# A linear-attention scan and a gated feed-forward layer on one core: v in two transfers, and three PSUM banks for the second layer from its first unit

## The chip, the cores and the metric

One core of a Trainium2 chip. The metric is the device time of one launch in microseconds (us), the median of three runs; lower is better. Five engines are programmed: TensorE (PE, matmuls; its weight loads are PEld), VectorE (DVE), ScalarE (ACT), GpSimd (POOL) and SyncE (SP, which here only issues DMAs). Each engine runs its instructions in the order in which the program gives them to it, and waits on semaphores for the others.

## The reference, cut to what matters

```python
# r, k, v: (4, 8, 768, 48); w, u: (8, 48)
for t in range(S):
    cur = einsum('bhd,bhe->bhde', u * kt, vt)
    y[:, :, t] = einsum('bhd,bhde->bhe', rt, state + cur)
    state = w * state + einsum('bhd,bhe->bhde', kt, vt)
x = y.transpose(0, 2, 1, 3).reshape(4, 768, 384)
h = maximum(x @ w_in, 0)                  # 384 -> 1024
conv_out = 3-tap convolution of h along the sequence, a weight per channel
out = (h * sigmoid(conv_out)) @ w_out     # 1024 -> 384
```

## The kernel before

The scan is done in 24 groups g of 128 tokens (4 batch elements of 6 groups; two chunks of 64 tokens in each). `load(g)` brings k and r with the head dimension on the partitions (tile KR, two transfers of 48 or 64 rows), v with the tokens on the partitions (tile TOK), and from g = 11 (NE) on also k and r with the tokens on the partitions (`in_krt`, into TOK). v lies in memory with zeros beside it, in blocks of [128 rows, 2, 384]; rows 0 to 63 need block 0 and rows 64 to 127 block 1, 1,536 bytes a row. `prep(g)` multiplies KR by decay factors (`TKR`, made once at the start in the PSUM bank PO2; `TKS` is its copy in SBUF), makes the scaled k (for g < 11 by matmuls, line 453) and the diagonal of the scores. `visit(g, av, su)` is the scan itself: scores of the next group (SP, line 516), outer products k by v of the next group (UP, line 525), and outputs of this group (AV, lines 521 and 527). Its outputs go to XT; from g = 3 on, six small SBUF-to-SBUF transfers of a group ("mv", line 560) put the last head in place.

The feed-forward layer goes in seven units u of up to 462 columns, and eight blocks f of 128 channels: `first` makes nine matmuls into HP (line 585), then ACT and DVE do the convolution and the gate, and the result is split into two parts GG (ten buffers). `second` makes three matmuls for each of three output blocks m (line 626), and accumulates over f in the PSUM banks PO0 to PO2. In units u < PH (two of them) only m = 0 and 1 follow each f; m = 2 follows for all eight f at the end of the unit, in bank PO0, since PO2 still holds the decay factors. The weights are converted piece by piece in unit 0 (`convert`: one DMA of 384 KB into one of three staging tiles ST, two ACT steps, one on DVE, one more on ACT, one on DVE or POOL).

The program lists all steps with what they read and write; a planner (`Plan.order`) with a cost for each step and a due time then writes out one order for all engines, and puts matmuls on zeros (line 699, "fillers") into PE gaps that it expects. Most steps go through helpers, so their lines in the profile are 292 (`tt`, an elementwise operation) and 295 (`dma`). Which step it is, is told by the tiles: KR<-KR,PO is the multiplication by the factors in PSUM, KR<-KR,TKR by those in SBUF.

Of the kernel before, what the change touches and what calls it, by code (L numbers as in the profile page):

```python
# [14 lines left out]
B, H, S, D = 4, 8, 768, 48  # L15
DM, DF = 384, 1024
C = 64
NP = H // 2
# [18 lines left out]

NE = 11
NX = 3
GP = 11  # L40
PH = 2
NBUF = 4
NT = 4
NO = 2
# [17 lines left out]
class Plan:  # L62
# [11 lines left out]
    def op(self, eng, dur, rd, wr, fn, cls="", x=0.0, port=False, mode=0, dma=False):  # L74
        n = len(self.ops)
        self.dma.append(dma)
        pred = set()
        for k in rd:
            if k in self.last_w:
                pred.add(self.last_w[k])  # L80
        for k in wr:
            if k in self.last_w:
                pred.add(self.last_w[k])
            pred.update(self.last_r.get(k, ()))
        for k in rd:
            self.last_r.setdefault(k, []).append(n)
        for k in wr:
            self.last_w[k] = n
            self.last_r[k] = []
        pred.discard(n)  # L90
        if not isinstance(dur, dict):
            dur = {eng: dur}
        cls = cls or (wr[0] if isinstance(wr[0], str) else wr[0][0])
        self.ops.append((dur, x, sorted(pred), fn, cls, mode))
        self.port.append(port)
        return n
# [134 lines left out]
def rwkv_ffn_kernel(tc, krd, krt, vt, wd, ut, w_in, conv_w, w_out, out):  # L231
    nc = tc.nc
    V, A, G, SP, PE = nc.vector, nc.scalar, nc.gpsimd, nc.sync, nc.tensor
    plan = Plan()
    op = plan.op
    with ExitStack() as ctx:
# [3 lines left out]
        def sb(shape, dt, name, n=None):  # L240
            if n is None:
                return cst.tile(shape, dt, name=name)
            return [cst.tile(shape, dt, name=f"{name}{i}") for i in range(n)]
# [3 lines left out]
        TOK = sb([128, 3, NP, 2, D], F32, "TOK", NBUF)  # L247
        SC = sb([128, NP, 2, C], F32, "SC", 2)
# [17 lines left out]
        TKS = sb([112, 2, NP, C], F32, "TKR")  # L266
# [9 lines left out]
        TKR = PO[2][0:112].rearrange("q (a p t) -> q a p t", a=2, p=NP)  # L276
# [11 lines left out]
        def tt(eng, n, rd, wr, cls="", psum=0, **kw):  # L288
            d = {"dve": dve(n, psum=psum), "pool": pool(n)}
            if eng != "any":  # L290
                d = {eng: d[eng]}
            op(eng, d, rd, wr, lambda e: e.tensor_tensor(**kw), cls, port=not psum)  # L292

        def dma(rd, wr, dst, src, dur=0.5, x=0.1, cls="", q="sp"):
            op(q, dur, rd, wr, lambda e: e.dma_start(dst, src), cls, x, dma=True)  # L295
# [11 lines left out]
        def kr(i):  # L307
            return [(n, i, x) for n in ("KK", "RR") for x in range(2)]
# [3 lines left out]
        def load(g, q="sp"):  # L312
            i = g % NBUF
            dst = KR[i].rearrange("q a p t -> q (a p t)")
            n = 64 if g < NBUF else D
            dma([], [(n_, i, 0) for n_ in ("KK", "RR")], dst[0:n], rows[g * 112 + 64:g * 112 + 64 + n], 0.45, 0.63, "ldK")
            dma([], [(n_, i, 1) for n_ in ("KK", "RR")], dst[64:64 + D], rows[g * 112:g * 112 + D], 0.45, 0.63, "ldK", q)
            if g >= NE:
                dma([], [("tK", i), ("tR", i)], TOK[i][:, 0:2], krt[g], 0.45, 1.3, "ldT")
            a = vt[g]  # L320
            v = bass.AP(a.tensor, a.offset, [[(64 * 2 + 1) * NP * 2 * D, 2], [2 * NP * 2 * D, 64], [1, NP * 2 * D]])
            dma([], [("tV", i)], TOK[i][:, 2].rearrange("q p c d -> q (p c d)"), v, 0.45, 0.65, "ldV")

        load(0, "act")
        dma([], ["uu"], uu, ut, 0.45, 0.4, "ldU")
        op("pool", 0.1, [], ["ident"], lambda e: G.memset(ident, 1.0))
# [23 lines left out]
        TKK = ["TK1", "TK2", "TR1", "TR2"]  # L350
# [22 lines left out]
        op("pool", 0.6, ["w64", "ident"], ["D64"], lambda e: G.tensor_tensor(  # L373
            out=D64, in0=ident.unsqueeze(1).broadcast_to([112, NP, D]), in1=w64.broadcast_to([112, NP, D]), op=ALU.mult))
        op("pe", 0.4, ["uu", "eye"], ["AV"], ucol, "ucol", 100, mode=1)
        op("act", 0.55, TKK, ["TKS"], lambda e: A.copy(TKS, TKR), "TKS")
        su_ = AV.rearrange("q p c t -> q (p c t)")[0:112, 0:NP].unsqueeze(2)
        op("dve", 0.2, ["AV", "PW"], ["uw"], lambda e: V.tensor_tensor(out=uw.unsqueeze(2), in0=su_, in1=PW[:, :, 1:2], op=ALU.mult))

        def decays():  # L380
            op("dve", 0.6, ["PW", "PW0"], ["PL"], powers2)
            op("act", 0.32, ["PL"], ["DN"], lambda e: A.copy(DN, PL[:, :, ::-1]))
            op("pe", 0.4, ["DN", "ident"], ["SUs"], th, "th", 350, mode=1)
            op("act", 0.4, ["SUs"], ["TH"], lambda e: A.copy(TH, SP_.rearrange("q p c t -> q (p c t)")[:, 0:NP * D].rearrange("q (p d) -> q p d", p=NP)))
# [44 lines left out]
        def prep(g):  # L429
            i = g % NBUF  # L430
            k_t, r_t = TOK[i][:, 0], TOK[i][:, 1]
            kr_ = KR[i][0:112].rearrange("q a p (c t) -> q (a p) c t", c=2)
            src = TKR if g < GP else TKS
            tkr = src.rearrange("q a p t -> q (a p) t").unsqueeze(2).broadcast_to([112, 2 * NP, 2, C])
# [4 lines left out]
            else:  # L439
                tt("dve", 1024, TKK if g < GP else ["TKS"], kr(i), "KR", int(g < GP), out=kr_, in0=kr_, in1=tkr, op=ALU.mult)  # L440
            s = SC[g % 2]
# [43 lines left out]
        def state(n):  # L485
            return ST_[n % 4]

        def visit(g, av, su):
            i, j = g % NBUF, (g + 1) % NBUF
            gj = (g + 1) % GPB  # L490
            rd, wr = [], []
            first = av and g % GPB == 0
            direct = g < NX
            if av:
                rd += [("SC", g % 2), ("tV", i), ("S", (2 * g + 1) % 4)] + kr(i) + ([] if first else [("S", 2 * g % 4)])
                wr += ["AV"]
            if su:
                rd += kr(j) + [("tK", j), ("tV", j)]
                wr += ["SUs", "SUu"]

            def outs(c, p):
# [27 lines left out]
            if su:  # L529
# [5 lines left out]
                for c in range(2):  # L535
# [3 lines left out]
                    a, b = state(n + c), state(n + c + 1)  # L539
# [7 lines left out]
            if av:  # L547
                b, gi = divmod(g, GPB)
                a = COLS * (b % 2) + gi * GT + (1 if b % 2 == 0 else 0)
# [63 lines left out]
        def second(i, m):  # L613
            u, f = divmod(i, NF)
            segs = UNITS[u][0]
            n = sum(s[2] + 2 for s in segs) - 2
            gi = i % NGB
            g2 = (GG[gi][:, 0, :n], GG[gi][:, 1, :n])
            ms = slice(m * 128, m * 128 + 128)
            k = m % 2 if u < PH else m  # L620
            po, key = PO[k], ("PO", k)
            dep = TKK if u == PH and m == 2 and f == 0 else []

            def mm(e):
                for j, (a, x) in enumerate(((0, 0), (0, 1), (1, 0))):
                    PE.matmul(po[:, :n], wo[a][:, f, ms], g2[x], start=(f == 0 and j == 0), stop=(f == NF - 1 and j == 2))  # L626
            op("pe", 3 * (n + 36) / 2400.0, [("wo", 0, f), ("wo", 1, f), ("GH", gi), ("GL", gi)], [key] + dep, mm, "f2", 3 * n)
            if f == NF - 1:
                q = nout[0] % NO
                nout[0] += 1  # L630
                o = OS[q][:, :n]
                op("act", act(n), [key], [("OS", q)], lambda e: A.activation(o, po[:, :n], AF.Copy, scale=1.0 / WS))
                col = 0
                for l, a, k in segs:
                    at = [(where(l, c), col + c - a) for c in range(a, a + k) if where(l, c) and (where(l, c), m) not in got]
                    col += k + 2
                    while at:
                        (b, t), c = at[0]
                        r = [x for x in at if x[0][0] == b]
                        at = at[len(r):]  # L640
                        got.update((x[0], m) for x in r)
                        dma([("OS", q)], [("out", u, m, b)], out[ms, b * S + t:b * S + t + len(r)], OS[q][:, c:c + len(r)], 0.45, len(r) / 700.0, "out")

        prep(0)
        conv_piece()
        visit(-1, False, True)
        for g in range(1, NBUF):
            load(g, "act" if g < 3 else "sp")
        done = [0]

        def visits(n):
            while done[0] < n:
                g = done[0]
                if g + 1 == NE:
                    decays()
                if g in SPLIT:
                    visit(g, True, False)
                if g + 1 < NG:
                    prep(g + 1)
                if g in SPLIT:  # L660
                    visit(g, False, True)
                else:
                    visit(g, True, g + 1 < NG)
                if g + NBUF < NG:
                    load(g + NBUF)
                done[0] += 1

        def behind(i):
            u, f = divmod(i, NF)
            for m in range(2 if u < PH else NM):  # L670
                second(i, m)
            if u < PH and f == NF - 1:
                for k in range(NF):
# [5 lines left out]
        for u in range(NU):  # L679
            a, b = UNITS[u][1], UNITS[u + 1][1] if u + 1 < NU else NG  # L680
            for f in range(NF):
                i = u * NF + f
# [80 lines left out]
```

## Time and profile before

| | |
|---|---|
| median of three runs | 357.77 us (355.97 to 359.85) |
| the profiled execution's own time | 360.75 us |
| its span, first to last instruction | 358.7 us |
| PE busy | 323.8 us, 90% of the span |
| DVE, ACT, POOL busy | 64%, 49%, 40% |
| mean granted TensorE clock | 0.916 |

PE is the engine with the most work, so time in which it waits, or runs at a low granted clock, is what can be won or lost. The granted clock is 1.00 at 2.4 GHz and 0.50 at 1.2 GHz. The shares are means over stages that differ: the start (to some 54 us), unit 0 with the conversion of the weights (54 to 108), units 1 to 4 with the rest of the scan (to 260), and the last units (to the end).

### The profile page before, as it was taken

How to read it: one execution, taken by the hardware profiler on the slowest of the kernel's cores; microseconds unless marked ns; L12 is line 12 of the kernel's file. 1: busy time of each engine (PE TensorE's matmuls, PEld its weight loads, DVE VectorE, ACT ScalarE, POOL GpSimd, SP SyncE). 2: the span in 40 equal slices, each digit the busy share in tenths (PEclk: the TensorE clock that was granted, in tenths of full speed). 3: DMA queues.
4: the chain of work that ended last, by engine and by line, in shares of the span. 5: the costliest groups of instructions: out<-in, count | busy, mean ns of one | idle time of the engine just before them, and what ended most of it. 6: DMA issues, size and time to landing. Idle time of an engine off the chain costs nothing.

```text
span 358.7 us, 11184 instructions
## 1 busy us (share of the span) xinstructions
PE 323.8 (90%) x4817; PEld 282.2 (79%) x4817; DVE 230.4 (64%) x372; ACT 174.6 (49%) x351; POOL 141.7 (40%) x157
## 2 busy tenths in 40 slices
PE   7499998977859999869999797999999999999993
PEld 4488887857758888758988686887988888889993
DVE  5234427958964756993878786669878764555551
ACT  3003117757854454443445355335464565666662
POOL 3001326735743362874452876444531021122320
PEclk9655579996996999998999999899999999999998
DMA  7442334573441513435524435244220002001001
GB/s 136 114 124 86 106 106 123 153 206 103 155 134 42 162 34 115 119 98 152 154 69 108 121 104 174 55 116 119 79 92 13 16 5 90 0 2 53 26 2 65
DMA packets 21297, 33.46 MB, mean 93 GB/s; under 512 B 4864, under 2 KB 15168, under 8 KB 21248
## 3 DMA queue, kind: packets, MB, share of 16 engines
q1 hardware_dynamic: 20960, 32.15, 30.8%
q10 hardware_dynamic: 288, 0.59, 0.8%
q8 instruction: 38, 0.62, 0.7%
q14 instruction: 11, 0.09, 0.1%
HBM read 25.95 MB, written 4.72 MB: 85 GB/s over the span
## 4 chain that ended last, share of the span: by engine, by line
PE 57%; DMA 18%; DVE 7%; POOL 6%; issue 5%; ACT 4%; SPq 2%; POOLq 0%; ACTq 0%
PE HP L585 20%; PE PO L626 20%; DMA TOK<-in_krt_dram 6%; DMA TOK<-in_vt_dram 5%; PE SP L516 4%; PE AV L527 3%; PE AV L521 3%; POOL TOK L292 2%; DVE ST L406 2%; DMA ST<-in_w_out_dram 2%; PE UP L525 2%; DMA ST<-in_w_in_dram 2%; SPq L295 2%; PE HP L461 1%; DVE CV L595 1%
## 5 line engine op out<-in xcount | busy, mean ns | idle before, releaser
L585 PE MATMUL HP<-XT,wi 128*128 128x464 f32 (+2 forms) x504 | 117.5, 379 | 8.2 <-DMA XT<-XT 3.6
L626 PE MATMUL PO<-GG,wo 128*128 128x462 f32 (+2 forms) x504 | 115.9, 371 | 6.1 <-POOL GG L292 4.8
L585 PEld LDWEIGHTS HP<-XT,wi 128*128 128x128 f32 x504 | 95.1, 196 | 18.8 <-DMA XT<-XT 3.8
L626 PEld LDWEIGHTS PO<-GG,wo 128*128 128x128 f32 x504 | 93.3, 191 | 18.3 <-POOL GG L292 6.4
L595 DVE SCALAR_TENSOR_TENSOR CV<-HP,cw,CV 128x462 f32<-128x462 f32 (+2 forms) x112 | 75.0, 670 | 33.5 <-ACT CV L592 32.7
L292 POOL TENSOR_TENSOR GG<-CV,GG 128x462 fp32r<-128x462 f32 (+2 forms) x35 | 39.7, 1135 | 71.9 <-ACT GG L601 61.0
L591 ACT ACTIVATE HP<-HP 128x464 f32<-128x464 f32 (+2 forms) x56 | 29.3, 523 | 54.6 <-PE HP L585 54.3
L527 PE MATMUL AV<-SC,TOK 64*48 64x64 f32 (+1 forms) x816 | 55.2, 235 | 0.0
L516 PE MATMUL SP<-KR 48*64 48x64 f32 x768 | 50.5, 244 | 3.6 <-ACT QQ L470 3.6
L599 DVE TENSOR_TENSOR CV<-HP,CV 128x462 f32<-128x462 f32 (+2 forms) x56 | 34.2, 611 | 28.6 <-ACT CV L598 28.3
L521 PE MATMUL AV<-KR,SS 48*48 48x64 f32 (+1 forms) x744 | 51.4, 235 | 0.9 <-issue 0.9
L516 PEld LDWEIGHTS SP<-KR 48*64 48x64 f32 x768 | 41.8, 147 | 10.7 <-issue 4.5
L525 PE MATMUL UP<-TOK 64*48 64x48 f32 x704 | 44.6, 218 | 4.6 <-DMA TOK<-in_vt_dram 4.6
L598 ACT ACTIVATE CV<-CV 128x462 f32<-128x462 f32 (+2 forms) x56 | 31.9, 569 | 27.2 <-DVE CV L595 27.1
L527 PEld LDWEIGHTS AV<-SC,TOK 64*48 64x48 f32 (+1 forms) x816 | 41.2, 132 | 0.4
L525 PEld LDWEIGHTS UP<-TOK 64*48 64x48 f32 x704 | 36.7, 136 | 5.2 <-issue 5.2
L521 PEld LDWEIGHTS AV<-KR,SS 48*48 48x48 f32 (+1 forms) x744 | 37.0, 130 | 2.5 <-issue 1.9
L601 ACT CAST GG<-CV 128x462 fp32r<-128x462 f32 (+2 forms) x56 | 31.1, 556 | 13.5 <-DVE CV L599 13.2
L292 POOL TENSOR_TENSOR MM<-SS,w 112x192 f32<-112x192 f32 x30 | 19.7, 657 | 42.1 <-DVE SS L292 22.9
L592 ACT ACTIVATE CV<-HP,cw 128x462 f32<-128x462 f32 (+2 forms) x56 | 35.2, 628 | 2.1
L292 POOL TENSOR_TENSOR TOK<-TOK 128x384 f32<-128x384 f32 x13 | 13.6, 1049 | 48.5 <-DMA TOK<-in_krt_dram 48.5
L555 ACT CAST XT<-AV 112x512 fp32r<-112x512 f32 (+1 forms) x24 | 13.8, 575 | 26.7 <-PE AV L527 26.1
(86 smaller groups left out, 335.0 us busy)
## 6 DMA issues: line engine op xcount, KB each, us to landing
KR<-in_krd_dram SPq DMA_DIRECT2D x41, 192.0 KB
TOK<-in_krt_dram SPq DMA_DIRECT2D x13, 384.0 KB
TOK<-in_vt_dram SPq DMA_DIRECT2D x24, 192.0 KB
ST<-in_w_in_dram SPq DMA_DIRECT2D x8, 384.0 KB
ST<-in_w_out_dram SPq DMA_DIRECT2D x8, 384.0 KB
XT<-XT SPq DMA_DIRECT2D x126, 16.0 KB
out_dram<-OS SPq DMA_DIRECT2D x6, 193.0 KB
out_dram<-OS SPq DMA_DIRECT2D x6, 191.0 KB
```

Of the source, the lines that this page charges most:

```text
L292: op(eng, d, rd, wr, lambda e: e.tensor_tensor(**kw), cls, port=not psum)
L516: PE.matmul(SP_[xs[x], p, c], KK[j][rows[x], p, t], RR[j][rows[x], p, t], start=True, stop=True)
L521: PE.matmul(o, state(2 * g + c)[rows[x]].rearrange("q p d -> q (p d)")[:, sc], RR[i][rows[x], p, t], start=True, stop=False)
L525: PE.matmul(UP[rows[x], n:n + D], TOK[j][xs[x], 0, p, c], TOK[j][xs[x], 2, p, c], start=True, stop=True)
L527: PE.matmul(o, TOK[i][xs[x], 2].rearrange("q p c d -> q (p c d)")[:, vc], SC[g % 2][xs[x], p, c], start=first and c == 0, stop=True)
L585: PE.matmul(hp, wi[a][:, j, fs], src(x, j), start=(j == 0 and k == 0), stop=(j == 2 and k == 2))
L592: op("act", act(n, 0, 1), [H_, "cw"], [("T", ti)], lambda e: A.activation(t1, hp[:, 1:n + 1], AF.Copy, scale=cw[:, 3 * f + 1:3 * f + 2]), ...
L595: op("dve", dve(n, psum=1) + 0.02, [H_, "cw"], [("T", ti)], lambda e, k=k: V.scalar_tensor_tensor(out=t1, in0=hp[:, k:n + k], scalar=cw[:, ...
L598: op("act", act(n, 1), [], [("T", ti)], lambda e: A.activation(t1, t1, AF.Sigmoid), "SG")
L599: op("dve", dve(n), [H_], [("T", ti)], lambda e: V.tensor_tensor(out=t1, in0=hp[:, 1:n + 1], in1=t1, op=ALU.mult), "GG")
L601: op("act", act(n, 1), [("T", ti)], [("GH", gi)], lambda e: A.copy(gh, t1), "GH")
L626: PE.matmul(po[:, :n], wo[a][:, f, ms], g2[x], start=(f == 0 and j == 0), stop=(f == NF - 1 and j == 2))
```

## The change

v is loaded by two transfers of 64 rows, each with its rows as the outermost dimension of both sides, in place of one whose source has the outermost dimension 2. PH goes from 2 to 0: m = 0, 1 and 2 follow each f in all units, in three banks. GP goes from 11 to 5: only groups 0 to 4 multiply by the factors in PSUM, groups 5 to 10 now too by the copy in SBUF. The copy itself (0.59 us of ACT) moves from the start to behind the preparation of group 2.

```diff
-GP = 11
-PH = 2
+GP = 5
+PH = 0
...
-            a = vt[g]
-            v = bass.AP(a.tensor, a.offset, [[(64 * 2 + 1) * NP * 2 * D, 2], [2 * NP * 2 * D, 64], [1, NP * 2 * D]])
-            dma([], [("tV", i)], TOK[i][:, 2].rearrange("q p c d -> q (p c d)"), v, 0.45, 0.65, "ldV")
+            for x in range(2):
+                xs = slice(x * C, (x + 1) * C)
+                dma([], [("tV", i, x)], TOK[i][xs, 2], vt[g, xs, x], 0.45, 0.3, "ldV")
...
-        op("act", 0.55, TKK, ["TKS"], lambda e: A.copy(TKS, TKR), "TKS")
...
-                rd += [("SC", g % 2), ("tV", i), ("S", (2 * g + 1) % 4)] + kr(i) + ([] if first else [("S", 2 * g % 4)])
+                rd += [("SC", g % 2), ("tV", i, 0), ("tV", i, 1), ("S", (2 * g + 1) % 4)] + kr(i) + ([] if first else [("S", 2 * g % 4)])
...
-                rd += kr(j) + [("tK", j), ("tV", j)]
+                rd += kr(j) + [("tK", j), ("tV", j, 0), ("tV", j, 1)]
...
+                if g + 1 == 3:
+                    op("act", 0.55, TKK + kr(2), ["TKS"], lambda e: A.copy(TKS, TKR), "TKS")
```

## Rows read from the trace of the kernel before

**Rows 1.** The page: busy time of each engine.
```profile
PE 323.8 (90%) x4817; PEld 282.2 (79%) x4817; DVE 230.4 (64%) x372; ACT 174.6 (49%) x351; POOL 141.7 (40%) x157
```

**Rows 2.** By stage: length, PE, PEld, DVE, ACT, POOL busy, PEclk, DMA share, GB/s.
```profile
0.00:9.10 9.10, 7.22 (x71) 3.73 (x71) 5.27 (x15) 3.53 (x8) 2.79 (x18) 1.00 0.69 134
9.10:13.70 4.60, 0.03 (x2) 0.03 (x1) 0.00 (x0) 0.00 (x0) 0.00 (x0) 0.80 0.32 91
13.70:49.40 35.70, 35.57 (x659) 31.08 (x661) 13.05 (x23) 5.69 (x15) 6.67 (x9) 0.50 0.39 111
49.40:54.00 4.60, 4.60 (x137) 4.19 (x134) 2.25 (x5) 0.82 (x2) 1.28 (x2) 1.00 0.37 94
54.00:108.00 54.00, 42.22 (x882) 36.98 (x880) 42.25 (x63) 36.89 (x85) 29.99 (x29) 0.93 0.49 147
108.00:162.00 54.00, 48.73 (x913) 42.10 (x913) 36.91 (x59) 25.47 (x50) 27.97 (x29) 0.94 0.33 97
...
180.00:260.00 80.00, 74.96 (x1138) 64.94 (x1137) 62.94 (x98) 38.38 (x71) 44.91 (x44) 0.98 0.37 105
260.00:345.00 85.00, 84.31 (x808) 76.29 (x807) 52.36 (x85) 50.80 (x97) 18.23 (x18) 1.00 0.10 31
```

**Rows 3.** The same for one short stretch at half the clock.
```profile
162.00:165.40 3.40, 3.40 (x9) 2.94 (x10) 0.00 (x0) 0.00 (x0) 1.69 (x2) 0.50 0.74 207
```

**Rows 4.** Waits of PE: who waited for whom, us in total, times, longest.
```profile
PE PO L626 <- POOL GG L292: 4.8, 4, 2.1
PE UP L525 <- DMA TOK<-in_vt_dram: 4.6, 1, 4.6
PE HP L585 <- DMA XT<-XT: 3.6, 1, 3.6
```

**Rows 5.** Chain that ended last: start, us, what (a DMA from issue to landing).
```profile
2.50 11.06 DMA TOK<-in_vt_dram
...
72.66 7.23 DMA ST<-in_w_in_dram
...
83.28 2.88 DMA ST<-in_w_out_dram
...
156.97 4.87 DMA XT<-XT
...
188.29 7.33 DMA TOK<-in_krt_dram
...
209.98 7.43 DMA TOK<-in_vt_dram
```

**Rows 6.** Timeline of SP, the DMA issues: start, us, tiles, count.
```profile
4.85 5.45 SPq L295 DMA_DIRECT2D KR<-in_krd_dram  x1
...
71.82 0.58 SPq L295 DMA_DIRECT2D TOK<-in_vt_dram  x1
...
154.38 0.57 SPq L295 DMA_DIRECT2D TOK<-in_vt_dram  x1
...
186.69 0.81 SPq L295 DMA_DIRECT2D KR<-in_krd_dram  x2
187.59 0.59 SPq L295 DMA_DIRECT2D TOK<-in_vt_dram  x1
188.29 0.40 SPq L295 DMA_DIRECT2D TOK<-in_krt_dram  x1
```

**Rows 7.** A stretch with one v transfer alone in flight: PE, PEclk, DMA share, GB/s.
```profile
34.40:37.60 3.20, 3.20 (x80) 0.50 0.14 49
```

**Rows 8.** The first burst of m = 2, a window of line 626.
```profile
120.72:125.14 4.42, 4.42 (x24) 4.10 (x24) 1.00 0.40 140
```

**Rows 9.** KR by the factors: groups by form; tile TKR (ns min/median/max).
```profile
L292 DVE TENSOR_TENSOR KR<-KR,TKR 112x1024 f32<-112x1024 f32 x13 | 18.1, 1392 | 1.5 <-DMA KR<-in_krd_dram 1.5
L292 DVE TENSOR_TENSOR KR<-KR,PO 112x1024 f32<-112x1024 f32 x8 | 9.7, 1211 | 0.0
...
L292 DVE TENSOR_TENSOR KR<-KR,TKR x13: 1206/1216/2042, 124.5 to 257.3; 112x1024 f32<-112x1024 f32 x13
```

## The prediction

> **What bounds the kernel now.** I read the page first: PE is busy 323.8 us, 90% of the span of 358.7 [rows 1], so about 35 us of idle PE time, and whatever its granted clock costs, are all that there is to win. The busy time by stage says where. At the start PE waits 4.6 us with no other engine busy, and then works without a gap from 13.7 to 49.4 us at half the clock (0.50, 1.2 GHz) [rows 2]. In unit 0 (54 to 108 us) it is idle for 54 − 42.2 = 11.8 us, while DVE is busy 78% and ACT 68%. From 108 to 162 it is idle 5.3 us, from 180 to 260 5.0 us, and from 260 on hardly at all (84.3 of 85) [rows 2]. So an idle microsecond of PE that goes anywhere before 260 is a microsecond of the end, as long as another wait doesn't take its place. The waits of PE and the chain that ended last name the causes: the first v transfer (4.6 us), a transfer XT<-XT (3.6 us), and GG parts that POOL delivers late (4.8 us) [rows 4].
>
> The chain also shows what the DMAs have in common. A v transfer of 192 KB takes 7.43 us from issue to landing, the first one 11.06, while a weight piece of 384 KB took 2.88 us [rows 5]. While one v transfer is alone in flight, the 16 DMA engines are busy 0.14 of the time, which is the time of 16 × 0.14 = 2.2 engines, and move 49 GB/s [rows 7]: 196.6 kB at that rate are 4.0 us. And what is issued behind a v transfer is slow too: w_in 0.8 us after v takes 7.23 us, krt 0.7 us after v 7.33, XT<-XT 2.6 us after v 4.87 [rows 5, 6].
>
> **v in two transfers.** The source of the old transfer has the outermost dimension 2, that of the new ones 64. If v then spreads as a weight piece does, it lands no later than one, 2.9 us for twice the bytes, and what stands behind it loses 7.2 − 2.9 = 4.3 us (w_in) and up to 4.4 (krt) [rows 5]. The Trainium skill, DMA: Bandwidth & Descriptors, has two rules here that disagree on this change. "Rules for kernel authors" says of two transfers to disjoint partition halves not to bother, since both share all 16 engines: by that rule v would gain nothing, and its result stands among the rivals. "Why a DMA increments its semaphore by 16 and not by 1" says that the slowest dimension of both sides decides over how many engines a transfer is spread, 2 before and 16 after. The 0.14 agrees with the second.
>
> SP gets 24 more issues. One of 128 rows took 0.57 to 0.59 us, one of KR's 48 rows 0.81 / 2 = 0.40 [rows 6], so a group costs SP 2 × 0.40 − 0.58 = 0.2 us more. XT<-XT and krt, issued behind v, start that much later; it is paid out of the 4 us that they win. An issue can also be held up: KR at 4.85 us took 5.45 us to issue behind two v transfers [rows 6], which should mostly go.
>
> Terms, against the 360.75 us of the profiled execution:
> - **Start.** The wait of 4.57 us for v ends at most. uu, KR and the first v are all asked for in the first 3 us, and moving at 134 GB/s [rows 2], so I keep 0.4 us of it: −4.2. The clock was 1.00 up to 9.1 us and 0.80 on the mean over the 4.6 us of waiting, so it fell some 2.8 us into the wait [rows 2]. These 2.8 us at full clock now do work that later took 5.5: up to −2.8, I take −1.5, since the KR of group 1 must be there too.
> - **Unit 0.** The chain goes through w_in at 72.66 us: −4.3 if nothing is next. DVE at 78% is next, so I take −3.5 for this and the other pieces, between 0 and 6.
> - **XT<-XT** at 156.97: PE waited 3.6 us. No row has this transfer without a v ahead, so between 0 and −3.6; I take −2.5. PE was idle before its clock fell to 0.50 for the 3.4 us from 162 [rows 3]; without the idle time half of this goes: −1.7.
> - **krt, 180 to 260.** The three idle stretches add up to 5.0 us [rows 2], the krt lands some 4 us earlier each time, POOL's work behind it stays. Between 0 and −5, I take −4. One of them is followed by a second stretch of 3.4 us at half the clock like that of [rows 3]: −1.7.
>
> **Three banks from the first unit on.** The matmuls are the same; the two bursts of m = 2, the first of 24 matmuls and 4.4 us [rows 8] and a second like it in unit 1, are cut in pieces of three matmuls (4.4 / 8 = 0.55 us) and moved up into unit 0 and unit 1, where PE idles 11.8 and 5.3 us. What falls into idle time is free: −8.8 us if all does, 0 if each piece only pushes the next `first` back. With part of that idle time already spent above, I take −2 in unit 0 and −1 in unit 1. At the end of unit 0 and of unit 1 there are now three output copies at once; the waits for that in the later units are covered by the 84.3 of 85 us [rows 2], so nothing.
>
> **Factors in SBUF from group 5 on.** Six multiplications read two SBUF operands instead of one. Undisturbed this costs nothing (1,216 against 1,211 ns), but the mean is 1,392 and the longest 2,042 [rows 9]: between 6 × 0 and 6 × 0.83 = 5.0 us of DVE, I take the mean, 6 × 0.18 = +1.1 us, and put it at full price, since it falls into unit 0 and just behind it. The Trainium skill, SBUF — State Buffer, "Who interferes with whom", says that a DVE instruction with two SBUF inputs contends with a GpSimd instruction that reads SBUF, and that one fully blocks; the spread from 1,206 to 2,042 agrees, and it is this rule that speaks against this part. The copy TKS leaves ACT at the start for a place where ACT is busy 5.7 of 35.7 us [rows 2]: nothing; if that cover were gone, its 0.59 us.
>
> **Sum.** −4.2 − 1.5 − 3.5 − 2.5 − 1.7 − 4 − 1.7 − 2 − 1 + 1.1 = −21.0 us. The profiled execution took 360.75 us (span 358.7 and 2.05 around it), 3 us over the median of 357.77. Taken off the median: **337 us**.
>
> **Rivals.**
> - **The clock stays up in the start.** From 13.7 to 49.4 us PE has 35.6 us of work at half the clock. If v is there in time, PE need not idle between 9.1 and 13.7, and the clock may not fall. For it: the matmuls from 49.4 to 54 us, of the same kinds, ran at 1.00 [rows 2]. Against: once it had fallen, a PE without a gap didn't raise it for 35 us, and at full clock the chain through DVE, ACT and POOL would open gaps. The work would take 17.8 us; with a quarter lost to gaps, 13 us are won on top: 324 us. Chance 0.25.
> - **Other waits take over.** In unit 0 DVE and ACT, and later POOL, may end last anyway. Then the start (5.7) and the two stretches of 1.7 us or so remain, with a little of krt: some −9 us, 349 us. For it: DVE's 78% [rows 2], and PE's 4.8 us of waits for POOL [rows 4]. Chance 0.17.
> - **Slower.** The new mechanism is DVE and POOL blocking each other in groups 5 to 10: at 0.83 us each, and the same again for POOL steps that are pushed back behind them, 6 × 0.83 × 2 = 10 us in the stage that is bound by DVE. It decides as soon as that chain, and not the DMAs, paces unit 0, so that of v's gains only the 5.7 us of the start are left: 357.8 − 5.7 + 10 = 362 us. Against: the rows of the same multiplication with the median at 1,216 ns. Chance 0.04.
> - **v gains nothing.** By the rule on halves, or because the new transfers are cut into runs of 192 bytes: no term but banks and factors stays, −3 + 1.1, less 24 × 0.2 us of SP if it shows: about 357 us. Against it the krt transfer, written in the same unflattened way, issued in 0.40 us [rows 6]. Chance 0.04.
>
> **How the numbers follow.** The forecast has 0.50. The range goes from the clock staying up (324, a little more if gaps are fewer) to the other waits taking over (349, a little more): 322 to 351 us, which leaves out the last two rivals and the tails. A measurement of this kernel can tell about 1% (3.6 us) from no change. The first three cases named (0.50, 0.25, 0.17) are all faster by more; of their tails I move 0.01: faster 0.91, same 0.05, slower 0.04.
>
> **What would show it.** Right: v lands within some 3 us of its issue where it stands alone, and the windows of DMA while it flies are no longer at 0.14; PE's first UP matmul starts at about 9 us; no PE wait on in_vt or XT<-XT; krt in about 3 to 4 us; no PE windows of 24 matmuls of line 626; KR<-KR,TKR 19 times. The granted clock from 12 to 45 us decides between the forecast and the first rival. Wrong: DVE's or ACT's share of unit 0 near 90% with the stage as long as before (second rival), or KR<-KR,TKR with a mean near 2 us (third). The planner writes a new order for all engines from the changed list; I can't cost that from this trace, and it is the most likely source of an error of a few microseconds either way.

## The result and the profile after

The changed kernel takes **323.81 us** (median of four runs, 320.92 to 327.64) against 358.32 us of the kernel before on the same chip (four runs, 355.97 to 359.85): ratio 0.9015, 95% interval 0.8927 to 0.9104. The forecast was 337 us with a range from 322 to 351. The result lies inside it, near its lower end, where the rival "the clock stays up in the start" had put 324 us. Ratios here and below are of the runs within 1.5% of the fastest of their kernel. A second measurement of the same kernel, further down, gave 0.9373 (0.9259 to 0.9487), and the two intervals don't meet. The profiled execution took 323.20 us, its span is 321.5 us, its mean granted clock 0.990.

The page, busy time of each engine and the granted clock in 40 slices, against [rows 1]:

```profile
PE 302.2 (94%) x4819; PEld 264.3 (82%) x4819; DVE 231.4 (72%) x368; ACT 174.6 (54%) x351; POOL 150.3 (47%) x161
PEclk9999899999999999999999999999999999999997
```

PE is busy 21.6 us less with the same matmuls (323.8 before), and idle 321.5 − 302.2 = 19.3 us in place of 34.9. The two numbers are the two kinds of gain: the same work at a higher clock, and fewer waits. Together they are the 37.2 us between the spans.

By stage (length, PE, PEld, DVE, ACT, POOL busy, clock, DMA share, GB/s). The stages are cut at the first matmul of a unit, so they end earlier than those of [rows 2]:

```profile
9.10:13.70 4.60, 3.80 (x127) 3.65 (x124) 2.62 (x5) 0.32 (x1) 0.51 (x1) 1.00 1.07 244
9.10:38.80 29.70, 26.98 (x790) 23.39 (x788) 14.78 (x27) 6.51 (x17) 7.45 (x11) 0.94 0.62 158
38.80:87.30 48.50, 42.64 (x876) 37.63 (x872) 43.82 (x65) 37.96 (x85) 29.83 (x27) 1.00 0.58 161
87.30:137.00 49.70, 48.61 (x948) 41.81 (x949) 40.28 (x58) 24.13 (x49) 31.91 (x32) 1.00 0.38 108
137.00:216.00 79.00, 77.67 (x1263) 67.92 (x1261) 66.00 (x106) 42.18 (x79) 50.37 (x50) 1.00 0.46 130
216.00:308.00 92.00, 91.61 (x847) 83.19 (x844) 57.23 (x92) 55.71 (x105) 25.98 (x25) 1.00 0.12 36
```

The kernel before, cut at the same matmuls, has unit 0 from 53.5 to 108.2 us, unit 1 to 162.0, units 2 and 3 to 252.7. Set side by side (us):

| stage | length before | after | PE busy before | after | PE idle before | after |
|---|---|---|---|---|---|---|
| start | 53.5 | 38.8 | 46.9 | 33.8 | 6.6 | 5.0 |
| unit 0 | 54.7 | 48.5 | 42.7 | 42.6 | 12.0 | 5.9 |
| unit 1 | 53.8 | 49.7 | 48.7 | 48.6 | 5.1 | 1.1 |
| units 2, 3 | 90.7 | 79.0 | 85.7 | 77.7 | 5.0 | 1.3 |
| units 4 to 6, tail | 106.0 | 105.5 | 99.7 | 99.4 | 6.3 | 6.1 |

The first row of the view after is the stretch in which PE had done 0.03 us of work in 4.6 [rows 2]; it now does 3.80. The clock, 0.50 from before 13.7 to 49.4 us there, is 1.00 in the changed kernel up to 318 us except for the 3.4 us from 31.5. The matmuls of the start, the same 859, thus take 13.1 us less of PE's time. Behind the start, the kernel before had four more stretches at half the clock, at 80, 107, 162 and 223 us, with 4.64, 5.96, 3.40 and 3.40 us of busy PE; half of that is 8.7 us. The changed kernel has none of them. 13.1 + 8.7 = 21.8 us make up the 21.6 us of busy time. Unit 0 and unit 1 are as busy as before because m = 2 has moved forward: of the second layer's matmuls 54 lie in unit 0 against 36, and 142 in units 2 and 3 against 162.

The waits of PE, against [rows 4] (who waited for whom, us, times, longest):

```profile
PE HP L584 <- DMA XT<-XT: 2.8, 2, 1.4
PE PO L625 <- POOL GG L292: 2.4, 3, 0.9
...
PE UP L524 <- DMA TOK<-in_vt_dram: 0.8, 1, 0.8
```

v: 4.6 us before, 0.8 now. XT: 3.6 to 2.8, now in two waits. GG, POOL's late parts: 4.8 to 2.4; POOL itself waited 48.5 us for krt before and 13.5 now, so that is a late DMA too, one step further back.

The chain, against [rows 5], and the issues by transfer (KB each, median us to landing):

```profile
3.02 6.78 DMA TOK<-in_vt_dram
...
52.79 3.99 DMA ST<-in_w_out_dram
...
76.46 1.61 DVE KR L292
...
83.33 3.10 DMA XT<-XT
...
126.40 2.35 DVE KR L292
...
135.16 3.81 DMA XT<-XT
```

```profile
KR<-in_krd_dram SPq DMA_DIRECT2D x41, 192.0 KB, 3.6
TOK<-in_krt_dram SPq DMA_DIRECT2D x13, 384.0 KB, 3.7
TOK<-in_vt_dram SPq DMA_DIRECT2D x48, 96.0 KB, 3.4
ST<-in_w_in_dram SPq DMA_DIRECT2D x8, 384.0 KB, 3.7
```

No v, w_in or krt behind the start is left among the long pieces of the chain; their medians are 3.4 to 3.7 us, where [rows 5] has single ones of 7.2 to 7.4. The first v still takes 6.78 us.

KR by the factors, against [rows 9]:

```profile
L292 DVE TENSOR_TENSOR KR<-KR,TKR 112x1024 f32<-112x1024 f32 x19 | 28.1, 1479 | 2.0 <-DMA KR<-in_krd_dram 2.0
L292 DVE TENSOR_TENSOR KR<-KR,PO 112x512 f32<-112x512 f32 x6 | 3.9, 681 | 2.6 <-DMA KR<-in_krd_dram 2.6
L292 DVE TENSOR_TENSOR KR<-KR,PO 112x1024 f32<-112x1024 f32 x2 | 2.4, 1214 | 0.6 <-ACT TKR L654 0.6
```

19 with the SBUF factors, as foreseen; all of them together take 34.4 us (28.1 + 3.9 + 2.4) against 31.7 before, 2.7 more where 1.1 was put in the sum. Two of the 19 stand in the chain above, with 1.61 and 2.35 us against 1.21 for one from PSUM: up to 1.5 us of the end.

### The profile page after: what moved, and what is told of

It is laid out like the page before. It is cut to its first block, busy times and chain, and to the rows that moved or that the text cites. A ratio compares the mean times of both kernels' runs of the same rounds, so it can differ in the third digit from the quotient of the medians.

```text
span 321.5 us, 11217 instructions
## 1 busy us (share of the span) xinstructions
PE 302.2 (94%) x4819; PEld 264.3 (82%) x4819; DVE 231.4 (72%) x368; ACT 174.6 (54%) x351; POOL 150.3 (47%) x161
## 4 chain that ended last, share of the span: by engine, by line
PE 73%; DMA 7%; DVE 7%; ACT 3%; issue 3%; SPq 3%; POOL 2%; POOLq 0%; DVEq 0%; ACTq 0%
PE HP L584 27%; PE PO L625 26%; PE SP L515 5%; PE AV L526 4%; PE AV L520 3%; SPq L295 3%; PE UP L524 2%; DMA XT<-XT 2%; DMA TOK<-in_vt_dram 2%; DVE ST L405 2%; DMA KR<-in_krd_dram 1%; PE SP L460 1%; DMA ST<-in_w_out_dram 1%; DVE KR L292 1%; POOL wo L292 1%
## 5 line engine op out<-in xcount | busy, mean ns | idle before, releaser
L584 PE MATMUL HP<-XT,wi 128*128 128x464 f32 (+2 forms) x504 | 113.3, 368 | 5.0 <-DMA XT<-XT 2.8
L584 PEld LDWEIGHTS HP<-XT,wi 128*128 128x128 f32 x504 | 91.6, 188 | 15.4 <-issue 1.7
L292 POOL TENSOR_TENSOR GG<-CV,GG 128x462 fp32r<-128x462 f32 (+2 forms) x37 | 44.7, 1208 | 75.5 <-ACT GG L600 67.0
L526 PE MATMUL AV<-SC,TOK 64*48 64x64 f32 (+1 forms) x816 | 49.6, 220 | 1.1 <-issue 1.0
L598 DVE TENSOR_TENSOR CV<-HP,CV 128x462 f32<-128x462 f32 (+2 forms) x56 | 34.4, 614 | 21.0 <-ACT CV L597 20.2
L520 PE MATMUL AV<-KR,SS 48*48 48x64 f32 (+1 forms) x744 | 46.4, 221 | 0.1
L515 PE MATMUL SP<-KR 48*64 48x64 f32 x768 | 45.2, 228 | 1.1 <-ACT QQ L469 1.1
L515 PEld LDWEIGHTS SP<-KR 48*64 48x64 f32 x768 | 37.8, 133 | 7.2 <-issue 4.7
L524 PE MATMUL UP<-TOK 64*48 64x48 f32 x704 | 40.2, 204 | 0.8 <-DMA TOK<-in_vt_dram 0.8
L526 PEld LDWEIGHTS AV<-SC,TOK 64*48 64x48 f32 (+1 forms) x816 | 37.5, 121 | 1.5 <-issue 1.3
L524 PEld LDWEIGHTS UP<-TOK 64*48 64x48 f32 x704 | 33.1, 122 | 1.5 <-issue 0.9
L292 DVE TENSOR_TENSOR KR<-KR,TKR 112x1024 f32<-112x1024 f32 x19 | 28.1, 1479 | 2.0 <-DMA KR<-in_krd_dram 2.0
```

Of the source, the lines that this page charges most:

```text
L515: PE.matmul(SP_[xs[x], p, c], KK[j][rows[x], p, t], RR[j][rows[x], p, t], start=True, stop=True)
L520: PE.matmul(o, state(2 * g + c)[rows[x]].rearrange("q p d -> q (p d)")[:, sc], RR[i][rows[x], p, t], start=True, stop=False)
L524: PE.matmul(UP[rows[x], n:n + D], TOK[j][xs[x], 0, p, c], TOK[j][xs[x], 2, p, c], start=True, stop=True)
L526: PE.matmul(o, TOK[i][xs[x], 2].rearrange("q p c d -> q (p c d)")[:, vc], SC[g % 2][xs[x], p, c], start=first and c == 0, stop=True)
L584: PE.matmul(hp, wi[a][:, j, fs], src(x, j), start=(j == 0 and k == 0), stop=(j == 2 and k == 2))
L598: op("dve", dve(n), [H_], [("T", ti)], lambda e: V.tensor_tensor(out=t1, in0=hp[:, 1:n + 1], in1=t1, op=ALU.mult), "GG")
```

## The experiments

The theory: a v transfer whose source has the outermost dimension 2 moves on some two DMA engines, is late itself, and delays what is issued behind it; halves with 64 rows outermost spread. The rivals: the banks or the factors bring the gain, or the new order does; and for the start, that something other than v decides the clock. Twelve kernels ran in three groups of four, each group on a chip of its own together with the kernel before, whose medians were 359.71, 359.70 and 355.48 us.

### v alone

The changed kernel with the old banks, factors and place of the copy:

```diff
-GP = 5
-PH = 0
+GP = 11
+PH = 2
```

> Only v by two transfers; PH = 2, GP = 11 and the place of the TKS copy as before. My theory (the spread of v over the DMA engines does nearly all of it, and with it the clock stays up in the start): 326 to 334 us, first matmul of unit 0 at about 39 us instead of 53.5, granted clock 1.00 from 5 to 30 us. Rival (the three banks from the first unit on, with the new order, do at least half of it): 340 us or more.

Measured: 335.8 us (329.39 to 340.19), ratio 0.9288 (0.898 to 0.9596), a median above the 326 to 334 us expected and below the rival's 340. Most of the gain is there with v alone; against the second measurement of the changed kernel (0.9373) it would be all of it. The granted means were 0.976 in the shortest run and 0.936 in the longest, and in the profiled run the start lost its clock:

```profile
13.70:42.80 29.10, 28.47 (x549) 24.32 (x547) 10.54 (x20) 5.24 (x14) 6.17 (x8) 0.53 0.40 108
```

PE waited 1.0 us for v in this run, against 0.8 in the changed kernel and 4.6 before, and yet the clock fell at 15.5 us. Unit 0 begins at 46.9 us. So an early v is not enough for the clock.

### Banks and factors alone

The kernel before with GP = 5, PH = 0 and the copy behind group 2; v as before.

> Only PH = 0, GP = 5 and the moved TKS copy; v by the one transfer of before. My theory: 352 to 358 us, the wait of some 4.6 us for the first v and the clock at 0.50 from 12 to 49 us as before, no bursts of 24 matmuls. Rival (banks): 345 us or less.

Measured: 368.09 us (366.47 to 369.09), ratio 1.033 (1.0198 to 1.0462): slower, by an interval that only just takes in 2%, and against the expectation. PE's waits (QQ is the diagonal of the scores, OS the output copies, CV the convolution):

```profile
PE HP L584 <- DMA XT<-XT: 5.2, 2, 3.9
PE PO L625 <- POOL GG L292: 5.1, 5, 1.5
PE HP L584 <- DVE CV L598: 4.8, 3, 2.3
PE UP L524 <- DMA TOK<-in_vt_dram: 4.2, 1, 4.2
PE PO L625 <- ACT OS L631: 3.1, 2, 2.7
```

The waits for XT and OS have grown (3.6 and 0.7 us before), those for v and GG have stayed. They are the smaller part of the loss: PE's idle time is 37.1 us (34.9 before) and its busy time 328.5 (323.8), so most of the 6.9 us between the two spans is work at half the clock. Behind the start this profile has six stretches at 0.50, from 3.4 to 6.8 us long, where before had four. The first reading was that the bursts of m = 2, now missing, had given PE something to do while DMAs were late. It is tested under "factors alone".

### The same program with v on few engines

Program, order, instructions and halves of the changed kernel; only v's source lies in memory with a gap after 32 rows, so that each half is written with the outermost dimension 2 (`g >= 0` holds for every group):

```diff
-                dma([], [("tV", i, x)], TOK[i][xs, 2], vt[g, xs, x], 0.45, 0.3, "ldV")
+                h = vt[g, x]
+                if g >= 0:
+                    h = bass.AP(h.tensor, h.offset, [[33 * 2 * NP * 2 * D, 2], [2 * NP * 2 * D, 32], [1, NP * 2 * D]])
...
+                dma([], [("tV", i, x)], TOK[i][xs, 2].rearrange("q p c d -> q (p c d)"), h, 0.45, 0.3, "ldV")
```

> The changed kernel with its list of steps, and so its order, unchanged; only the source of each half of v is laid out so that its outermost dimension is 2 (a gap of one row after 32 rows). My theory: each half is again slow, the DMA share with v alone in flight is again about 0.14, and the time is that of the banks alone, 350 to 358 us. Rival (it is the splitting in two, or the new order, that counts): 322 to 330 us.

Measured: 364.51 us (358.39 to 366.83), ratio 1.0134 (0.9717 to 1.0551), above the 350 to 358 us expected. The whole gain is gone, with every instruction in its place. A stretch with v alone in flight, PE's waits (the lines are five higher in this kernel), and two transfers of the chain that were issued behind a v:

```profile
34.10:35.60 1.50, 1.50 (x52) 1.33 (x52) 1.25 (x2) 0.00 (x0) 0.00 (x0) 0.50 0.13 47
```

```profile
PE PO L630 <- POOL GG L292: 10.6, 9, 3.2
PE HP L589 <- DMA XT<-XT: 5.0, 2, 2.7
PE UP L529 <- DMA TOK<-in_vt_dram: 4.1, 2, 2.0
```

```profile
88.28 7.23 DMA ST<-in_w_in_dram
...
203.98 7.40 DMA TOK<-in_krt_dram
```

Share 0.13 and 47 GB/s: the picture of [rows 7], from the outermost dimension alone. Also w_in and krt behind v take the 7.2 to 7.4 us of [rows 5] again. POOL waits 49.9 us for krt (13.5 in the changed kernel), which PE sees as GG. Sending two transfers instead of one is worth nothing by itself.

### Which v costs what

Only group 0 in the slow form (`if g == 0:` in place of `if g >= 0:` above), and only groups 4 to 23 (`if g >= NBUF:`).

> As the changed kernel, but the two halves of group 0 alone with the outermost dimension 2. If the early v is what keeps the clock up: PE waits some 3 to 5 us at 9 us, the clock falls to 0.50 for most of 12 to 45 us, and the time is 334 to 342 us. If the clock is kept up by something else: only the wait itself comes back, 326 to 329 us.

Measured: 339.44 us (339.07 to 342.69), ratio 0.955 (0.9406 to 0.9694). Windows of the start:

```profile
9.10:13.70 4.60, 0.20 (x5) 0.09 (x2) 1.98 (x3) 0.00 (x0) 0.00 (x0) 0.95 0.91 165
13.70:50.00 36.30, 34.30 (x631) 29.78 (x633) 11.03 (x20) 5.91 (x16) 6.68 (x9) 0.50 0.32 94
```

PE stands still for v and works on at half the clock: the start of before again [rows 2]. Unit 0 begins at 55.3 us, 16.5 later than in the changed kernel.

> As the changed kernel, but the halves of v of groups 4 to 23 with the outermost dimension 2; groups 0 to 3 spread. If start and later stages add up: the run with all halves on two engines lost 364.5 - 323.8 = 40.7 us, the one with group 0 alone 15.6, so this one should lose about 25 us: 345 to 352 us, unit 0 starting at 39 to 41 us, and late XT, krt and GG back among PE's waits. If the clock of the start sets everything behind it: below 335 us.

Measured: 348.62 us (344.19 to 354.13), ratio 0.9706 (0.9474 to 0.9938). PE's waits for GG are 9.0 us, for XT 3.8, POOL's for krt 46.5. In points of the ratio, the changed kernel lies at 90.2, the first v slow costs 5.3 more, the later ones 6.9, and all of them 11.2: within the intervals the two parts add up. The intervals are wide, and the parts aren't cleanly apart: unit 0 began at 45.6 us in the profiled run, not at 39 to 41, since the clock fell at 18.0 us although v of groups 0 to 3 was spread.

### One plain transfer

v stored without the block of zeros and read by one transfer with 128 rows outermost, in the order that the planner writes for it:

```diff
-            for x in range(2):
-                xs = slice(x * C, (x + 1) * C)
-                dma([], [("tV", i, x)], TOK[i][xs, 2], vt[g, xs, x], 0.45, 0.3, "ldV")
+            dma([], [("tV", i, 0), ("tV", i, 1)], TOK[i][:, 2], vt[g], 0.45, 0.6, "ldV")
```

> As the changed kernel, but v lies in memory without the zeros, and one plain transfer of 128 rows of 1,536 bytes brings it: 24 issues fewer on SP, and a list of steps (and an order) that differs a little. If the spread over the engines is what counts, and not that there are two transfers: 318 to 326 us. If the two halves matter: 335 us or more.

Measured: 333.35 us (331.61 to 336.45), ratio 0.9402 (0.9254 to 0.955), against the expectation of a time like that of the changed kernel. v lands in 3.2 us (median), so one transfer spreads as well as two; the units from unit 0 on have lengths like those of the changed kernel (47.5, 50.3, 40.1 us for the first three; there 48.5, 49.7, 39.8). What is lost is the start: unit 0 begins at 48.8 us, the clock was 0.50 from 17.4 to 44.7. Around the fall PE has a gap that no semaphore explains (start us, us, the operation, idle time before it and its cause):

```profile
17.93 0.80 PE L458 MATMUL HP<-uw,SC 48*64 48x1 f32 x12 [2.58 <-issue]
```

One packet of 16 KB of instructions was under way from 15.4 to 16.5 us; the DMA share was 0.95 in the 1.4 us ahead of it and 0.54 in the gap. To tell the order from the transfer, the same source was put under the changed kernel's own order (the second of the two steps issues nothing):

> The changed kernel with its own order, but v by one plain transfer of 128 rows; the second of the two steps issues nothing. The plain transfer with an order of its own took 333 us, with the clock at 0.50 from 17 to 45 us. If that was the order: 319 to 326 us here. If it is how full the DMA queues are at 10 to 16 us (transfers issued earlier, in front of PE's code loading at 15.4 us): again 330 to 336 us, with a gap of PE of 1 us or more near 16 us.

Measured: 329.63, 331.54 and 332.85 us, ratio 0.9443 (0.9282 to 0.9603); a fourth run took 486.81 us at a mean clock of 0.553, is left out of the ratio and stays unexplained. Unit 0 begins at 48.0 us:

```profile
9.00:12.60 3.60, 2.87 (x96) 2.72 (x95) 1.98 (x3) 0.32 (x1) 0.23 (x1) 1.00 1.09 289
12.60:43.00 30.40, 29.94 (x553) 25.50 (x552) 11.03 (x20) 5.67 (x15) 6.44 (x9) 0.50 0.40 105
```

So it isn't the order. The gap isn't the cause either: here the clock fell at 12.6 us, and the only gap near 16 us was one of 0.33 us at 17.6. Why one plain transfer comes with a fallen clock is open.

### Without the fillers

The 31 matmuls that the planner puts into PE's idle time in the start are left out. The planner also writes another order without them (VectorE has 378 instructions in place of 368, GpSimd 151 in place of 161):

```diff
-        fill, hist = True, []
+        fill, hist = False, []
```

> As the changed kernel without the 31 filler matmuls on zeros. If it is the early v together with the fillers of the first 30 us that keeps the clock up: the clock falls to 0.50 by 12 us and the time is 332 to 338 us. If the early v alone does it: 320 to 326 us.

Measured: 333.2 us (332.75 to 335.49), ratio 0.9401 (0.9285 to 0.9517); all four runs have a mean clock of 0.931 to 0.933.

```profile
9.00:11.40 2.40, 1.39 (x45) 1.37 (x47) 1.67 (x3) 0.00 (x0) 0.00 (x0) 1.00 1.08 249
11.40:45.00 33.60, 32.72 (x652) 29.87 (x649) 15.95 (x27) 10.58 (x25) 9.08 (x10) 0.50 0.48 131
```

The clock falls at 11.4 us here, and by the mean clocks it fell in all four runs. The median is 9.4 us above the first measurement of the changed kernel and 3.2 above the second. Whether it is the fillers that hold the clock, or the order, this run doesn't tell: PE had done 1.39 us of work in the 2.4 us ahead of the fall, against 1.60 in the changed kernel, but in the run before this one 2.87 in the 3.6 us ahead of its fall, against 2.80 in the changed kernel, which kept its clock.

### Factors alone, and factors without a new order

The kernel before with GP = 5 and the copy moved, but the bursts kept (PH = 2):

> The kernel before with GP = 5 and the moved TKS copy, PH = 2 as before: the bursts stay, and six multiplications of KR read the factors from SBUF. The banks alone were 8 us slower than before. If DVE and POOL blocking each other in groups 5 to 10 is the reason: 364 to 370 us. If it is that the bursts of m = 2 are missing as cover for late transfers: 355 to 361 us.

Measured: 367.76 us (365.25 to 370.28), ratio 1.0338 (1.0165 to 1.051), the same loss as with the banks. The bursts are there, so a loss of this size doesn't need their absence. The two kernels differ in PH alone, so beside a slow v three banks bring nothing and cost nothing (368.09 against 367.76 us). PE's waits:

```profile
PE SP L515 <- ACT QQ L469: 9.5, 3, 4.1
PE HP L584 <- DMA XT<-XT: 4.8, 2, 2.9
...
PE PO L625 <- ACT OS L631: 4.2, 5, 2.4
```

Other waits than under the banks (QQ 9.5 us here, 3.0 there, 3.6 before), for the same sum; again more of it is busy time (329.7 us, 323.8 before) than idle time (38.5, 34.9). Then the kernel before in its own order, in which groups 5 to 10 merely read the other operand:

```diff
-            src = TKR if g < GP else TKS
+            src = TKR if g < 5 else TKS
```

> The kernel before with its own order of all instructions; only the operand of KR's multiplication in groups 5 to 10 is the copy in SBUF. The factors alone were 8 us slower than before. If DVE and POOL blocking each other is the reason, the loss stays: 364 to 369 us. If it is the new order that the planner wrote for the changed list, it goes: 355 to 361 us.

Measured: 360.26 us (356.77 to 364.17), ratio 1.0207 (1.0039 to 1.0376).

```profile
L292 DVE TENSOR_TENSOR KR<-KR,TKR 112x1024 f32<-112x1024 f32 x19 | 26.8, 1412 | 2.1 <-DMA KR<-in_krd_dram 2.1
```

The mean of 1,412 ns is that of before (1,392), QQ is back at 3.6 us, and GG has 6.9 (4.8). Two of its runs, at mean clocks of 0.918 and 0.924, took 358.41 and 356.77 us; the kernel before took 361.14, 355.48 and 357.33 us at 0.916 to 0.924. At the same clock nothing is seen, and no stage of the profiled run is longer than before (53.2, 54.2, 52.6, 90.3 and 106.0 us, against the table's 53.5, 54.7, 53.8, 90.7 and 106.0). The 4.8 us between the medians are an upper bound, and three runs of before at 0.941 or 0.942 make most of them. So at equal clocks the 8 us that the two kernels above lost came with the order that the planner wrote anew, the place of the copy included; by the medians alone, at least 3 of the 8.

### The bursts with the fast v, and the changed kernel again

> The changed kernel with PH = 2: v and the factors as changed, but m = 2 of units 0 and 1 in bursts as before. If three banks from the first unit on are worth what the prediction gave them (3 us): 325 to 330 us. If more, by way of the idle time of units 0 and 1: above 332. If nothing: 321 to 325 us.

The changed kernel with PH = 2. Measured: 338.33 us (330.46, 337.4, 339.26, 339.87). Its profiled run is the one of 330.46, which the other three, at mean clocks of 0.933 to 0.948, don't reach: the clock stayed up in the start, unit 0 begins at 37.5 us, unit 1 is 53.3 us long (49.7 in the changed kernel). Behind the first burst (from 134.5 us):

```profile
PE SP L515 <- issue: 3.0, 1, 3.0
```

> The changed kernel once more, beside the other three on the same chip: 320 to 328 us, clock 1.00 over most of the first 40 us. If its clock falls here in the start, as in the others: 330 us or more.

Measured: 329.96 us (327.51 to 331.58), ratio 0.9373 (0.9259 to 0.9487). The profiled run, 330.96 us, has the fallen clock and unit 0 at 46.1 us. Its windows, and after them those of the first profiled run of the same kernel:

```profile
9.00:15.00 6.00, 5.28 (x153) 4.82 (x152) 4.06 (x7) 0.80 (x2) 1.01 (x2) 1.00 1.03 243
15.00:42.00 27.00, 26.87 (x521) 23.12 (x519) 8.96 (x17) 5.21 (x14) 5.65 (x7) 0.50 0.36 102
```

```profile
9.00:15.00 6.00, 5.20 (x148) 4.66 (x148) 3.92 (x7) 0.80 (x2) 1.01 (x2) 1.00 1.06 241
15.00:31.50 16.50, 14.58 (x469) 12.21 (x469) 9.10 (x17) 5.23 (x14) 4.93 (x7) 1.00 0.51 136
```

The six microseconds ahead of the fall are the same to 0.1 us of busy PE, and in one run the clock fell and in the other it didn't. Two of the eight runs of this kernel have a mean clock of 0.953 to 0.958 (330.96 and 331.58 us), the other six 0.980 to 0.991 (320.92 to 328.97 us). So the kernel sits at an edge: by the mean clocks the same code keeps the clock in most runs and loses it in some, and in the profile where it is lost unit 0 begins 7.3 us later (46.1 against 38.8).

## Why the prediction was right

**v.** The mechanism was right as put: spread, not size or number of transfers, sets v's time and that of its followers. The same program with the two-engine form is back at 1.0134 of before. The Trainium skill, DMA: Bandwidth & Descriptors, had a rule for each side; the 0.13 and 47 GB/s agree with "Why a DMA increments its semaphore by 16 and not by 1". The rule on halves, in "Rules for kernel authors" of the same page of the Trainium skill, was the basis of the rival "v gains nothing", which has fallen; what it says of halves agrees with the plain transfer, which lands in 3.2 and 3.8 us in its two kernels against 3.4 for halves. The old single transfer wasn't of that kind.

**The idle terms** were right in sum: 4.2 + 3.5 + 2.5 + 4 + 3 − 1.1 = 16.1 us predicted, 34.9 − 19.3 = 15.6 measured. Those of v alone were 14.2, and the run with v alone has 34.9 − 20.8 = 14.1. By stage: unit 0 6.1 (3.5 and 2 of the banks), unit 1 4.0 (2.5 and 1), units 2 and 3 3.7 (4). The start gave only 1.6 of its 4.2: the wait for v shrank by 3.8 us, but a PE at full clock now has gaps behind it, as the first rival had said. The wait for XT<-XT, put at −2.5 and named as one that should go, shrank only from 3.6 to 2.8 us. That misses of this size cancel in the sum is luck.

**The clock terms** are the step that was mis-sized: 1.5 + 1.7 + 1.7 = 4.9 us predicted, 21.6 measured in the profiled run. 13.1 of them are the start, where the forecast had the clock fall (1.5 us) and the first rival (0.25) had it stay. The sentence that a PE without a gap had not raised it for 35 us was right and beside the point: with v early, it need not fall. The other miss are the stretches at 80 and 107 us, worth 2.3 and 3.0 us, which had no term; the two with a term, at 162 and 223, gave the 1.7 us each that they were put at. That the result meets the rival's 324 us so closely is luck: it had 4.2 + 1.5 + 13 = 18.7 us for the start, which gave 53.5 − 38.8 = 14.7, and the stretches without a term made up for it. For a run in which the clock does fall the forecast holds better: 337 against the 330.96 and 331.58 us of the two such runs.

**Banks and factors** were put at −3 + 1.1, the banks by way of idle time. The profiles, compared from unit 0 to the end so that the clock of the start is left out, show another size and another way. With the fast v and bursts this stretch took 290.7 us (v alone) and 291.0 (factors too); with three banks 282.7 and 283.1 (the two profiles of the changed kernel). So with the fast v the banks are worth some 8 us and the factors nothing that is seen; 8.4 us is also what lies between the medians of the changed kernel with and without bursts (338.33 and 329.96). Only some 2 us of the 8 are idle time. The rest is PE's busy time (273.4 and 274.2 against 268.4 and 268.1): both profiles with bursts have three stretches at half the clock behind the start, of 3.4 to 6.8 us, and those with three banks have none before 318 us. These are single profiles, in orders that the planner wrote for each list; why the clock falls there isn't settled. With the slow v the same stretch took 305.2 us before, 314.5 with the factors and 312.7 with the banks as well: a loss, with the factors' new order, to which the banks add nothing. The remark that the new order couldn't be costed from the trace was the right warning, and 8 us is its measured size. It isn't settled which step of the order does it; the waits that grow are those for XT, QQ and OS, different ones in the two kernels.

**The rivals.** "Other waits take over" fell: DVE went from 78% to 43.82 / 48.5 = 90% of unit 0, but the mark that the prediction had named was 90% with the stage as long as before, and the stage became 6.2 us shorter. "Slower" by DVE and POOL blocking fell: KR's mean is 1,479 ns, not 2,042. The Trainium skill, SBUF — State Buffer, "Who interferes with whom", agrees in direction with that mean against 1,214 ns from PSUM. As a cost of the end it is at most the 1.5 us of the two multiplications in the chain, near the 1.1 us of the sum; in the order of the kernel before none is seen.

## What to carry to other kernels

Look at the DMA share while one transfer is alone in flight: at 0.14 it runs on about two engines, and what is queued behind it pays too; rewrite the access pattern so that the outermost dimension is long on both sides. An order written around late transfers is not a neutral background: the banks brought nothing beside the slow v and some 8 us beside the fast one, and the factors came with a loss of 8 us beside the slow v alone, so test such parts together and apart. Look at PE's busy time beside its waits: most of what these parts lost and won was work at half the clock, which no list of waits shows. Where TensorE's clock falls because of one early wait, price both outcomes, since the clock may be worth more than the wait: here the wait shrank by 3.8 us, and two profiles of the changed kernel with and without a fallen clock differ by 7.3 us at the beginning of unit 0.

## What the runs showed of the hardware that was not expected

- The granted clock is not a function of the program alone: with 5.20 and 5.28 us of PE work in the same 6 us it stayed at 1.00 in one run and went to 0.50 for 27 us in another.
- PE stood still for 2.6 us (one plain transfer, from 15.35 us) and 3.0 us (bursts with the fast v, from 134.5 us) with no semaphore to wait for, while a 16 KB packet of instructions was in flight for 1.1 us of it. The fourteen profiles have nine such gaps of more than 0.8 us, and in all nine PE goes on 1.3 to 1.6 us after a packet of instructions has ended. That PE waited for its code fits this well, but it is argued, not shown. That the data transfers made the code late isn't borne out: the DMA share in the two gaps is 0.54 and 0.29, and in one of 1.05 us in the changed kernel (from 19.03 us) it is 0.00.
- One transfer of 128 rows and two of 64 land alike (3.2 and 3.4 us), and yet the plain one had a fallen clock in the start in both profiles, with mean clocks from 0.942 to 0.959 in seven of its eight runs (0.553 in the one of 486.81 us), and the halves in one profile of two of the changed kernel. This is open.
